# Attention and two feed-forward blocks on one core: the early weight decoding pinned in ScalarE's queue and paced, the turned operands of the second block begun later, one more piece behind the last product

## The chip, the cores and the metric

The kernel runs on one core of a Trainium2 chip. The metric is device time of one execution in microseconds (us), the median of several executions. Engine names in the rows: PE is TensorE's matmul, PEld its weight load, DVE is VectorE, ACT is ScalarE, POOL is GpSimd, SP is the engine whose queue issues nearly all DMAs here.

## What is computed

```python
# q, k, v: 4 batches x 8 heads x 576 positions x 64; window 128, one slope per head
scores = where(0 <= rel < 128, q @ k.T / sqrt(D) - slope * rel, -1e9)
attn   = softmax(scores) @ v                       # -> x: 2304 tokens x 512
y      = ((x @ w_a) * (x @ w_b)) @ w_out           # moe:  d_ff = 1536
h      = y @ w_in2                                 # moe2: d_ff = 2048
g      = where(h >= 1, h, where(h <= -1, 0, (h + 1)**2 / 4))
out    = g @ w_out2                                # 2304 x 512
```

The weights come as 64-bit numbers; the kernel turns each tile of them into float32 words on chip, and then into a high and a low part, so that three matmuls stand for one product.

## The kernel before

**Stages.** First the attention, with the first four of twelve column blocks of the first feed-forward block computed beside it, half a block of tokens (256) at a time: `attention()` yields after each step, `products()` after each group of three or twelve matmuls, and the loop at the end of the kernel runs them against each other by the table `PACE`. Then `after_attention()`: seven visits, a plain one that ends the first four column blocks for the last tokens, three visits for the other eight blocks of the first feed-forward block, and three for the second. In those six a product of 2x2 blocks is done as seven products (`seven_steps`), whose operands are sums of blocks of the tokens, made ahead by `x7_first` and `x7_second` ("turned"). The last visit splits its down product in seven too, but for its last pair of blocks, which is done plainly by `close7_pieces`.

**Early decoding.** Beside the attention, `early_job(key)` decodes 22 further weight tiles (`EARLY`), whose words go to memory until the later stages want them. `fetch` loads the raw tile (512 KB) on SP's queue. `words` then does two ACT instructions, `e = |high half|` and `up = low half * 2^-29`, and three DVE instructions; `total_bits` adds `e` and `up` on DVE, and a DMA stores `e` (256 KB, line 694). One step of a job runs with each step of `products()` (`WE = 1`), and a job has six. There are three buffers for raw tiles, two for `e` (`EB = 2`) and two for `up`; so the ACT instruction that writes `e` of a tile needs the store of the tile two before it to have landed, and a raw load needs the tile three before it to have been read. `fetch_next` keeps `FETCH` raw tiles on their way.

**Order.** In the attention stage a scheduler decides the order in each engine's queue, by priority and by when it takes inputs to be there. In the later stages PE's order is that of the code (`manual_schedule`), and the scheduler orders the other engines. Each queue runs in order: an instruction that waits holds up what stands behind it. `background` runs the later decoding and the turned operands beside the matmuls, one step of the latter after each product (`BG`), `after` lets out the pieces of the down products at a rate per product. In the last pair of the last visit that rate is lowered by `LAG / 7` a product, so that pieces are left over to stand between the last product and `close7_pieces`, which needs the last product's result.

**`x7_second`** makes the turned operands of the second block for one block of tokens, in two halves: a load of `xf` (line 928), then the first DVE subtraction on it (line 931), and further sums and splits.

Of the kernel before, what the change touches and what calls it, by code (L numbers as in the profile page):

```python
# [9 lines left out]
F32 = mybir.dt.float32  # L10
# [3 lines left out]
AF = mybir.ActivationFunctionType  # L14
# [12 lines left out]
def attention_and_two_ffns(  # L27
# [12 lines left out]
    nc = tc.nc  # L40
# [53 lines left out]
    YB = 4  # L94
    EARLY = 22
    EFROM = 1
    WE = 1
    HOLD = 3
    PRI = 300
    ET = mybir.EngineType  # L100
# [5 lines left out]
    BG = [(3, 2, 24), (3, 1, 24), (1.5, 1, 19), (2, 1, 12), (3, 1, 0), (3, 1, 0), (2, 1, 0)]  # L106
    VISITS = [(1, 0), (1, 1), (1, 2), (2, 0), (2, 1), (2, 2)]
    FLIP = [0, 1, 0, 0, 1, 0]
    FETCH = 2
    ABS = 'AA'  # L110
    D7 = ((2, 2),)
    GN = 11
# [5 lines left out]
    E_PC = 'V'  # L118
    E_W = 'P'
    CORD = ((1, 0), (0, 0), (0, 1), (1, 1))  # L120
    LAG = 2
    E_PV = 'V'
    TQ = 3
    TN = 3
    HP = lambda n: n < HPN
    const = ctx.enter_context(tc.tile_pool(name="const", bufs=1))
    xp = ctx.enter_context(tc.tile_pool(name="xp", bufs=1))
# [351 lines left out]
    state = {"w": 0, "credit": 0.0}  # L479
# [35 lines left out]
            count["e"] = count.get("e", 0) + 1  # L515
            fetch(coming.popleft(), "w64" if count["e"] % 3 or FETCH < 2 else "w64c")

    def words(key):

        pool, be, bu = (later["dec"], EB2, UB2) if later else (wdec, EB, UB)  # L520
        if key not in raws:
            fetch(key)
        raw = raws.pop(key)
        word = raw.bitcast(U32).rearrange("p (n two) -> p n two", two=2)
        lo, hi = word[:, :, 0], word[:, :, 1]
        e = pool.tile([P, 4 * P], U32, tag="e", name="e", bufs=be)
        up = pool.tile([P, 4 * P], U32, tag="up", name="up", bufs=bu)
        ef = e.bitcast(F32)
        if ABS[bool(later)] == "A":
            nc.scalar.activation(ef, hi.bitcast(F32), AF.Abs)  # L530
            yield e, up
        nc.scalar.activation(up, lo, AF.Copy, scale=2.0**-29)  # L532
        yield e, up
        if ABS[bool(later)] == "A":
            nc.vector.tensor_scalar(ef, ef, W64_MIN, W64_MAX, ALU.max, ALU.min)
        else:
            nc.vector.tensor_scalar(ef, hi.bitcast(F32), W64_MIN, W64_MAX, ALU.abs_max, ALU.min)
        yield e, up
        nc.vector.tensor_scalar(e, e, 5, 2, ALU.logical_shift_left, ALU.logical_shift_right)
        yield e, up  # L540
        nc.vector.scalar_tensor_tensor(e, hi, 0xC0000000, e, ALU.bitwise_and, ALU.bitwise_or)
        yield e, up
# [133 lines left out]
    V = nc.vector  # L676
# [10 lines left out]
    coming = deque(ahead)  # L687

    def early_job(key):
        for e, up in words(key):  # L690
            yield
        total_bits(e, e, up)
        early[key] = dram.tile([P, 4 * P], F32, name=f"w32_{key[0]}{key[1]}")
        nc.sync.dma_start(early[key], e.bitcast(F32))
        fetch_next()
        yield
# [198 lines left out]
    def x_tile(name):  # L895
        return xp.tile([P, 2, BW], F32R, tag="x", name=name, bufs=NB * NC)

    def x7_second(b, where):

        t1, t2 = two()  # L900
        xs[b] = [x_tile(f"z{c}") for c in range(NC)]
        if where == "memory":
            parked[2, b] = {q: dram.tile([P, 2, 2, QW], F32, name=f"t2_{b}{q}") for q in (2, 3, 6)}
        else:
            turned[2, b] = {q: t_tile(where) for q in (2, 3, 6)}

        def split(hi, lo, src):
            nc.scalar.copy(hi, src)
            yield
            minus(V, lo, src, hi)  # L910
            yield

        def turn(q, c, src):
            if where != "memory":
                yield from split(*(turned[2, b][q][:, z, c] for z in range(2)), src)
                return
            while not room():
                yield "no room"
            me = ("turned2", b, q, c)
            take(me)  # L920
            t = w_tile("wt")
            yield from split(t[:, 0, :QW], t[:, 1, :QW], src)
            nc.sync.dma_start(parked[2, b][q][:, :, c], t[:, :, :QW].bitcast(F32))
            give(me)

        for c in range(2):
            f = xp.tile([P, 2, BW], F32, tag="x", name="xf", bufs=NB * NC)
            nc.sync.dma_start(f, xf[b][:, c])
            yield
            b11, b12, b21, b22 = f[:, 0, Q1], f[:, 0, Q2], f[:, 1, Q1], f[:, 1, Q2]  # L930
            V.tensor_tensor(t1, b12, b11, less_)
            yield
            V.tensor_tensor(t2, b22, t1, less_)
            yield
            V.tensor_tensor(b12, b22, b12, less_)
            yield
            yield from turn(3, c, t1)
            yield from turn(2, c, t2)
            V.tensor_tensor(t1, b21, t2, less_)
            yield  # L940
            for k in range(2):
                x = xs[b][c + 2 * k]
                yield from split(x[:, 0], x[:, 1], f[:, k])
            yield from turn(6, c, t1)
        made.add((2, b))
        yield
# [576 lines left out]
    for need in products():  # L1523
# [7 lines left out]
        if not later and begun >= 0:  # L1531
            for _ in range(XE):
                if jobs_x:
                    run(jobs_x)
            if begun >= EFROM and ahead and not waiting and not jobs_w:
                jobs_w.append(early_job(ahead.pop(0)))
            for _ in range(WE):
                if jobs_w:
                    run(jobs_w)
        owed += PACE[min(begun, len(PACE) - 1)]  # L1540
# [33 lines left out]
```

## Time and profile before

| | |
|---|---|
| runs | 973.14, 975.70, 975.98 us; median 975.7 |
| the profiled execution's own time | 974.94 us |
| its span in the profile | 973.2 us, so 1.74 us lie outside the span |
| PE busy in the span | 937.1 us, 96% |
| DVE, ACT, POOL busy | 720.6, 565.0, 169.5 us |
| mean granted TensorE clock | 0.988 of 2.4 GHz |

A PE that is busy for 96% of the span can gain from a change only by its few idle stretches, and by those in which its clock is granted lower. The page's row by slices rounds both away, so stages are read by windows.

### The profile page before, as it was taken

The page shows a single profiled execution, that of the slowest core. Times are in us where ns is not written, and L with a number is a line of the kernel's source. Part 1 is how long each engine was busy: PE and PEld are TensorE (multiplying, and loading weights), DVE is VectorE, ACT ScalarE, POOL GpSimd, SP SyncE. Part 2 cuts the span into 40 slices and gives each one's busy share as a digit, 9 for nine tenths or more (in the row PEclk, how much of TensorE's full clock was granted, in tenths as well). Part 3 has the DMA queues.
Part 4 walks back from the last instruction along what each step waited for, and adds up shares of the span by engine and source line. Part 5 has one row for each costly group of instructions (what it writes and reads, how often), then busy time and mean ns, then how long its engine had stood idle before and what let it go on. Part 6 is the DMA issues. An engine that isn't in the chain of part 4 may idle for free.

```text
span 973.2 us, 18277 instructions
## 1 busy us (share of the span) xinstructions
PE 937.1 (96%) x6397; PEld 874.6 (90%) x6397; DVE 720.6 (74%) x1704; ACT 565.0 (58%) x1346; POOL 169.5 (17%) x311
## 2 busy tenths in 40 slices
PE   4999999899999999999999999999999999999997
PEld 3889889799999899999989999888888888899997
DVE  6698787794944988885677667899876656467886
ACT  6778676664433454353434435788775656586662
POOL 5567444344100000000000000000000000032233
PEclk9999999999999999999999999999999999999999
DMA  9967787830545888798868997876777776587851
GB/s 215 181 147 180 209 218 185 220 98 2 163 156 198 311 311 301 281 365 332 265 225 328 383 364 271 310 247 211 272 285 238 246 241 229 178 269 257 268 185 65
DMA packets 177580, 229.01 MB, mean 235 GB/s; under 512 B 92880, under 2 KB 132048, under 8 KB 177488
## 3 DMA queue, kind: packets, MB, share of 16 engines
q1 hardware_dynamic: 173680, 224.96, 70.9%
q10 hardware_dynamic: 3808, 2.88, 1.0%
q8 instruction: 51, 0.84, 0.3%
q14 instruction: 41, 0.34, 0.1%
HBM read 156.24 MB, written 71.57 MB: 234 GB/s over the span
## 4 chain that ended last, share of the span: by engine, by line
PE 71%; DVE 4%; DMA 3%; issue 1%; ACT 0%; SPq 0%; POOL 0%; DVEq 0%; POOLq 0%
PE mm L1027 32%; PE acc L1209 14%; PE acc L1148 10%; PE acc L1352 5%; PE mm L1117 3%; PE acc L642 1%; DMA xf<-xf 1%; DMA e<-w_b 1%; PE ps_s L348 1%; PE mm L593 1%; PE mm L595 1%; PE ps_o L412 1%; PE mm L594 1%; PE acc L1396 1%; PE ps_t L380 0%
## 5 line engine op out<-in xcount | busy, mean ns | idle before, releaser
L1256 POOL TENSOR_TENSOR h<-h,h 128x384 f32<-128x384 f32 x21 | 23.5, 1118 | 656.0 <-DVE h L1243 647.1
L1027 PE MATMUL mm<-xt,ws 128*128 128x384 f32 x612 | 124.5, 338 | 0.7 <-DVE a L968 0.7
L1027 PEld LDWEIGHTS mm<-xt,ws 128*128 128x128 f32 x612 | 106.8, 188 | 6.0 <-DVE a L968 1.3
L1027 PE MATMUL mm<-z,ws 128*128 128x384 f32 x480 | 97.2, 337 | 0.5 <-DVE h L968 0.5
L1027 PEld LDWEIGHTS mm<-z,ws 128*128 128x128 f32 x480 | 84.4, 188 | 5.3 <-DVE h L968 0.8
L1209 PE MATMUL acc<-ws,gh 128*128 128x512 f32 x252 | 79.0, 394 | 0.0
L369 POOL TENSOR_SCALAR s<-s,ssum 128x192 f32<-128x192 f32 (+2 forms) x144 | 69.8, 498 | 28.9 <-DVE ssum L364 20.9
L358 ACT ACTIVATE s<-s,nmax 128x192 f32<-128x192 f32 (+2 forms) x144 | 62.4, 437 | 16.2 <-DVE nmax L354 15.9
L1027 PE MATMUL mm<-x,ws 128*128 128x384 f32 x348 | 70.7, 338 | 0.3 <-ACT s L1048 0.2
L1148 PE MATMUL acc<-gh,ws 128*128 128x512 f32 (+1 forms) x224 | 65.3, 335 | 0.0
L1027 PEld LDWEIGHTS mm<-x,ws 128*128 128x128 f32 x348 | 61.7, 188 | 3.8 <-ACT s L1048 0.9
L530 ACT ACTIVATE e<-w 128x512 f32<-128x512 f32 x68 | 45.4, 672 | 33.8 <-DMA w_a<-e 6.3
L348 PE MATMUL ps_s<-kt,diag 128*128 128x192 f32 (+2 forms) x288 | 62.1, 337 | 2.0 <-ACT diag L176 0.9
L976 ACT CAST gh<-a 128x384 fp32r<-128x384 f32 x56 | 28.3, 513 | 56.8 <-DVE a L1056 37.9
L968 DVE TENSOR_TENSOR h<-mm,s 128x384 f32<-128x384 f32 x72 | 39.8, 553 | 27.7 <-PE mm L1027 27.6
L1352 PE MATMUL acc<-ws,go 128*128 128x256 f32 x423 | 58.9, 282 | 0.4 <-DVE sum L968 0.4
L593 PE MATMUL mm<-x,w 128*128 128x256 f32 x192 | 57.4, 304 | 0.1
L1352 PEld LDWEIGHTS acc<-ws,go 128*128 128x128 f32 x423 | 56.1, 189 | 1.5 <-DVE sum L968 1.3
L595 PE MATMUL mm<-x,w 128*128 128x256 f32 x192 | 57.0, 298 | 0.1
L532 ACT ACTIVATE up<-w 128x512 uint32<-128x512 uint32 x68 | 45.9, 675 | 19.2 <-DVE e L546 7.5
L594 PE MATMUL mm<-x,w 128*128 128x256 f32 x192 | 56.9, 297 | 0.0
L976 ACT CAST gh<-c 128x384 fp32r<-128x384 f32 x68 | 34.6, 512 | 37.4 <-PE acc L1209 29.9
(153 smaller groups left out, 2519.8 us busy)
## 6 DMA issues: line engine op xcount, KB each, us to landing
ws<-w_ii SPq DMA_DIRECT2D x57, 512.0 KB, 5.5
ws<-w_p SPq DMA_DIRECT2D x48, 512.0 KB, 4.5
ws<-w_ab SPq DMA_DIRECT2D x37, 512.0 KB, 6.3
w_p<-wb SPq DMA_DIRECT2D x30, 512.0 KB, 4.7
w<-in_moe_w_out_dram SPq DMA_DIRECT2D x28, 512.0 KB, 5.0
w_ab<-wb SPq DMA_DIRECT2D x24, 512.0 KB, 3.0
w_ii<-wb SPq DMA_DIRECT2D x24, 512.0 KB, 4.1
w<-in_moe_w_in_dram SPq DMA_DIRECT2D x16, 512.0 KB, 4.7
```

The lines of the kernel that those rows point to most:

```text
L348: nc.tensor.matmul(ps[:, z, c : 3 * D], qd[:, i - q0 // D, :], kt[:, (i - 2) * D + c - k0 : (i + 1) * D - k0], start=True, stop=True,)
L358: nc.scalar.activation(at(z, i), at(z, i), AF.Exp, bias=nmax[:, z : z + 1], scale=-1.0, accum_out=ssum[:, z : z + 1],)
L369: ENG[E_N[2 * b + (m >= 2)][z]].tensor_scalar(at(z, i), at(z, i), ssum[:, z : z + 1], 1.0, ALU.mult, ALU.mult)
L532: nc.scalar.activation(up, lo, AF.Copy, scale=2.0**-29)
L593: nc.tensor.matmul(ps, w[:, 0, cs], xh[c], start=(c == 0), stop=False)
L594: nc.tensor.matmul(ps, w[:, 0, cs], xl[c], start=False, stop=False)
L595: nc.tensor.matmul(ps, w[:, 1, cs], xh[c], start=False, stop=(c == NC - 1))
L976: nc.scalar.copy(hi[:, t_], src)
L1027: nc.tensor.matmul(ps, w[:, k, cs], operand(here, q, ci, m), start=q in (0, 1, 3) and ci + n == 0, stop=ci == 1 and n == 2, skip_group_che ...
L1148: nc.tensor.matmul(dst, w[:, i, cs], m[:, t_], start=first and k == 0 and (n < NC or c % 2 == 0), stop=last and k == 2 and (n < NC or c % ...
L1209: nc.tensor.matmul(v["acc"][n], m[:, ss], w[:, i], start=first and k == 0, stop=last and k == 2,)
L1352: nc.tensor.matmul(dst, g[a][:, ss], w[:, b], start=opens and n == 0, stop=closes and n == 2, skip_group_check=True,)
```

## The change

Four edits. **Pinned decoding:** the two ACT instructions of an early job are tied behind the instruction that the code issued to ACT just before (`keep_in_program_order`), so the scheduler can't place them ahead of it; one job step is run for three out of four steps of `products()` (`WE = 0.75`) in place of each; and `fetch_next` keeps three raw tiles on their way. The buffers stay three, two and two. **Later operands:** `x7_second` lets four products go by between the load of a half and the first subtraction on it, in place of one, and ties this subtraction behind what DVE was given before. **Closing pair:** `LAG` is 3, not 2.

```diff
-    WE = 1
+    WE = 0.75
-    FETCH = 2
+    FETCH = 3
-    LAG = 2
+    LAG = 3
+    PIN = True
+    XW = 4
+    PINX = True
...
-    def words(key):
+    def words(key, pin=lambda ins: ins):
...
-            nc.scalar.activation(ef, hi.bitcast(F32), AF.Abs)
+            pin(nc.scalar.activation(ef, hi.bitcast(F32), AF.Abs))
...
-        nc.scalar.activation(up, lo, AF.Copy, scale=2.0**-29)
+        pin(nc.scalar.activation(up, lo, AF.Copy, scale=2.0**-29))
...
-        for e, up in words(key):
+        for e, up in words(key, tc.keep_in_program_order if PIN else lambda ins: ins):
...
+    def pinned(ins):
+        return tc.keep_in_program_order(ins) if PINX else ins
...
             nc.sync.dma_start(f, xf[b][:, c])
-            yield
+            for _ in range(XW):
+                yield
...
-            V.tensor_tensor(t1, b12, b11, less_)
+            pinned(V.tensor_tensor(t1, b12, b11, less_))
...
-            for _ in range(WE):
+            state["thin"] = state.get("thin", 0.0) + WE
+            while state["thin"] >= 1.0:
+                state["thin"] -= 1.0
                 if jobs_w:
                     run(jobs_w)
```

**ACT's queue in the attention stage.** Before, from the softmax exponential (line 358) ahead of one early tile's `e` (line 530, tile `w64_2738`) to the next tile's `e` (`w64_2807`); line 532 is `up`, the others are evictions of the attention and of the products.

```order
L358 ACTIVATE s3_140,ssum_2533<-s3_140,nmax_2532 128x192
L530 ACTIVATE e_2826<-w64_2738 128x512
L176 CAST x11_111<-ps_o_2569 128x3x64
L176 CAST x11_111<-ps_o_2568 128x3x64
L622 CAST gh_2696<-a_sb_2652 128x256
L532 ACTIVATE up_2945<-w64_2807 128x512
L176 COPY pt_2663<-ps_t_2659 128x384
L176 CAST x21_115<-ps_o_2569 128x64
L176 CAST x21_115<-ps_o_2568 128x2x64
L358 ACTIVATE s0_134,ssum_2637<-s0_134,nmax_2636 128x64
L358 ACTIVATE s0_134,ssum_2637<-s0_134,nmax_2636 128x128
L530 ACTIVATE e_2944<-w64_2807 128x512
```

After the change, the two tiles that stand nearest to there (`w64_2716` and `w64_2838`); lines are three higher.

```order
L533 ACTIVATE e_2978<-w64_2716 128x512
L535 ACTIVATE up_2979<-w64_2716 128x512
L361 ACTIVATE s3_140,ssum_2946<-s3_140,nmax_2945 128x192 x2
L179 COPY pt_3009<-ps_t_3006 128x256
L361 ACTIVATE s0_134,ssum_2987<-s0_134,nmax_2986 128x192 x2
L625 CAST gh_3100<-a_sb_3028 128x256
L535 ACTIVATE up_3055<-w64_2838 128x512
L179 COPY pt_3046<-ps_t_3042 128x384
L533 ACTIVATE e_3054<-w64_2838 128x512
```

From one tile's `e` to the next there were two exponentials, and now there are four. Over all 22 tiles, the first `e` stood and stands behind exponential 54 of 144; the last stood behind exponential 119, and now stands behind the last, 144.

**DVE's queue where the second half of the first block's operands begins** (first feed-forward block, last of its visits). Before, line 931 stands ahead of the decoder's last sum (546), four sums into `xsum` and the two splits `gl` that PE's down product reads.

```order
L541 SCALAR_TENSOR_TENSOR e_6860<-w64_6858,e_6860 128x512
L1060 TENSOR_TENSOR a_6576<-mm_6534,a_6576 128x384
L1056 TENSOR_TENSOR a_6576<-a_6576,s1_6618 128x384
L931 TENSOR_TENSOR x32_6559<-xf_6864 128x384
L546 ISA e_6860<-e_6860,up_6861 128x1024
L968 TENSOR_TENSOR xsum_6498<-acc_5776,xsum_6498 128x512
L170 TENSOR_TENSOR gl_6648<-a_6576,gh_6647 128x384
L968 TENSOR_TENSOR xsum_6516<-acc_5777,xsum_6516 128x512
L933 TENSOR_TENSOR x32_6559<-xf_6864,x32_6559 128x384
L935 TENSOR_TENSOR xf_6864<-xf_6864 128x384
L170 TENSOR_TENSOR gl_6648<-a_6576,gh_6647 128x384
```

After the change the same place reads so (lines are seven higher here):

```order
L544 SCALAR_TENSOR_TENSOR e_6857<-w64_6855,e_6857 128x512
L1067 TENSOR_TENSOR a_6576<-mm_6534,a_6576 128x384
L1063 TENSOR_TENSOR a_6576<-a_6576,s1_6616 128x384
L549 ISA e_6857<-e_6857,up_6858 128x1024
L975 TENSOR_TENSOR xsum_6498<-acc_5776,xsum_6498 128x512
L173 TENSOR_TENSOR gl_6645<-a_6576,gh_6644 128x384
L975 TENSOR_TENSOR xsum_6516<-acc_5777,xsum_6516 128x512
L173 TENSOR_TENSOR gl_6645<-a_6576,gh_6644 128x384
```

The subtraction on the second load (now line 938) has gone 23 instructions further back. The first half's subtraction of the same block, 22 instructions ahead of this place, stands between the same instructions before and after.

**PE's queue at the last product** (line 1027, after it 1034), with the pieces of the seven-product down step (1352, after it 1359) and the first of the closing pair (1396, after it 1403). Before:

```order
L1027 MATMUL mm_11437<-xt_8902,ws_11326 128x384 x6
L1352 MATMUL acc_10338<-ws_11247,go_11396 128x256 x3
L1352 MATMUL acc_11587<-ws_11245,go_11396 128x256 x6
L1352 MATMUL acc_11595<-ws_11245,go_11396 128x256 x3
L1352 MATMUL acc_10336<-ws_11247,go_11426 128x256 x6
L1352 MATMUL acc_10338<-ws_11247,go_11426 128x256 x3
L1352 MATMUL acc_11611<-ws_11218,go_11391 128x256 x6
L1352 MATMUL acc_11619<-ws_11218,go_11391 128x256 x3
L1396 MATMUL acc_10337<-ws_11350,gh_11468 128x256 x2
```

After:

```order
L1034 MATMUL mm_11437<-xt_8902,ws_11326 128x384 x6
L1359 MATMUL acc_10335<-ws_11247,go_11396 128x256 x3
L1359 MATMUL acc_10338<-ws_11247,go_11396 128x256 x3
L1359 MATMUL acc_11587<-ws_11245,go_11396 128x256 x6
L1359 MATMUL acc_11595<-ws_11245,go_11396 128x256 x3
L1359 MATMUL acc_10336<-ws_11247,go_11426 128x256 x6
L1359 MATMUL acc_10338<-ws_11247,go_11426 128x256 x3
L1359 MATMUL acc_11611<-ws_11218,go_11391 128x256 x6
L1359 MATMUL acc_11619<-ws_11218,go_11391 128x256 x3
L1403 MATMUL acc_10337<-ws_11350,gh_11468 128x256 x2
```

Three matmuls of the down step have moved from ahead of the last product to behind it: 33 stand there now, 30 before.

## Rows read from the trace of the kernel before

**Rows 1.** Windows: busy us of each engine in a stretch, granted clock, DMA.

```profile
60.00:86.00 26.00, 23.94 (x229) 21.17 (x228) 23.98 (x78) 21.21 (x69) 18.80 (x34) 0.93 0.66 161
86.00:110.00 24.00, 24.00 (x271) 23.25 (x271) 21.32 (x75) 18.55 (x58) 15.23 (x28) 1.00 0.79 198
110.00:204.00 94.00, 82.98 (x885) 77.71 (x884) 74.32 (x248) 63.22 (x210) 39.63 (x91) 0.95 0.76 199
204.00:245.00 41.00, 41.00 (x521) 39.71 (x521) 24.85 (x100) 21.73 (x77) 17.90 (x47) 1.00 0.12 35
303.00:350.00 47.00, 46.08 (x260) 42.98 (x260) 36.60 (x75) 22.52 (x46) 0.00 (x0) 1.00 0.79 284
350.00:720.00 370.00, 366.95 (x1997) 341.34 (x1996) 290.26 (x583) 201.89 (x401) 0.00 (x0) 1.00 0.84 300
```

**Rows 2.** Timeline of PE, 108 to 123 us, its one stall.

```profile
116.88 2.06 PE L412 MATMUL ps_o<-pt,v 64*64 64x64 f32 x56 [2.02 <-ACT pt L176]
```

**Rows 3.** Timeline of ACT, 105 to 122 us.

```profile
111.25 0.67 ACT L530 ACTIVATE e<-w 128x512 f32<-128x512 f32 x1 [1.01 <-DMA w_a<-e]
...
115.35 0.66 ACT L530 ACTIVATE e<-w 128x512 f32<-128x512 f32 x1 [2.29 <-DMA w<-in_moe_w_a_dram]
...
116.48 0.35 ACT L176 COPY pt<-ps_t 128x256 f32<-128x256 f32 x1
```

**Rows 4.** ACT's waits from 60 to 225 us: total us, times, longest.

```profile
ACT e L530 <- DMA w_a<-e: 6.3, 4, 2.3
...
ACT e L530 <- DMA w_o<-e: 4.9, 4, 1.7
ACT up L532 <- DMA w<-in_moe_w_out_dram: 3.9, 2, 3.0
ACT e L530 <- DMA w<-in_moe_w_a_dram: 3.9, 2, 2.3
ACT e L530 <- DMA w_b<-e: 2.6, 3, 1.7
ACT e L530 <- DMA w<-in_moe_w_b_dram: 2.4, 1, 2.4
...
ACT up L532 <- DMA w<-in_moe_w_b_dram: 1.9, 1, 1.9
...
ACT up L532 <- DMA w<-in_moe_w_a_dram: 1.0, 2, 0.7
```

**Rows 5.** DMA issues, 60 to 225 us: count, KB each, median us to landing.

```profile
w<-in_moe_w_a_dram SPq DMA_DIRECT2D x8, 512.0 KB, 4.9
...
w_a<-e SPq DMA_DIRECT2D x8, 256.0 KB, 3.7
```

**Rows 6.** SP's waits, 60 to 225 us: a raw load, and the first later load.

```profile
SPq L710 <- DVE pt L178: 23.1, 1, 23.1
SPq L508 <- DVE e L541: 18.8, 7, 5.3
```

**Rows 7.** Chain that ended last, 300 to 336 us: start, us, what.

```profile
310.12 4.89 DMA e<-w_b
```

**Rows 8.** Timeline of DVE, 480 to 514 us: the two halves' first subtraction.

```profile
494.60 0.56 DVE L931 TENSOR_TENSOR x<-xf 128x384 f32<-128x384 f32 x1 [2.33 <-DMA xf<-xf]
...
506.70 0.56 DVE L931 TENSOR_TENSOR x<-xf 128x384 f32<-128x384 f32 x1 [0.81 <-DMA xf<-xf]
```

**Rows 9.** Timeline of PE, 484 to 512 us: its stalls.

```profile
497.21 1.33 PE L1027 MATMUL mm<-xt,ws 128*128 128x384 f32 x6 [0.73 <-DVE a L968]
...
510.99 0.50 PE L1148 MATMUL acc<-gl,ws 128*128 128x512 f32 x1 [1.47 <-DVE gl L170]
```

**Rows 10.** Timeline of PE, 938 to 974 us: behind the last product.

```profile
955.54 3.75 PE L1352 MATMUL acc<-ws,go 128*128 128x256 f32 x30
959.12 0.40 PE L1396 MATMUL acc<-ws,gh 128*128 128x256 f32 x2
960.77 0.39 PE L1396 MATMUL acc<-ws,gl 128*128 128x256 f32 x1 [1.25 <-DVE gl L170]
```

## The prediction

> **What bounds the kernel now.** PE does. I read the table of engines first, then windows by stage, then inside the stages what PE waited for, and last the waits of the engine that it waited for. In the stages from 350 us on PE stands idle for 3 us in 370 [rows 1]; nothing that shortens work on another engine pays there. The attention stage is different, and the windows cut it so that the reason shows. From 60 to 86 us and from 110 to 204 us PE is idle for 2.06 and 11.02 us, and its granted clock is 0.93 and 0.95 of 2.4 GHz. Between them, from 86 to 110 us, it has no idle time and a clock of 1.00, though the early decoding runs there at its full pace and DVE is 89% busy (21.32 of 24). From 204 to 245 us, with no early decoding left, it also has none [rows 1]. So neither the attention nor the amount of decoding holds PE up, but something that happens in some places of the decoding.
>
> What it is can be read at one stall. At 114.9 us PE waits 2.02 us for an eviction `pt` of ACT [rows 2]. ACT had been standing since 113 us at the `e` of an early tile, for its raw load, 2.29 us; that `pt` comes only behind it [rows 3]. At 111.25 us it had stood 1.01 us for a store, that of the tile two before, since `e` has two buffers [rows 3]. Summed over 60 to 225 us ACT waits 8 times for raw loads (3.9 + 3.9 + 2.4 + 1.9 + 1.0 = 13.1 us) and 11 times for stores (6.3 + 4.9 + 2.6 = 13.8 us) [rows 4], 26.9 us in all. PE pays twice: it stands still, and its clock is granted lower behind such a stop.
>
> What is there to be had: 13.1 us of idle time, and for the clock 0.07 x 26 + 0.05 x 94 = 6.5 us (a stretch at half of 2.4 GHz does half its work; the clocks have two decimals, so 0.6 us either way). Together 19.6 us.
>
> **Pinned decoding: raw loads.** Nothing is added or removed: the same 22 tiles, the same two ACT and four DVE instructions each, the same DMAs. What moves is seen in the queues. I count in softmax exponentials, which stand in every queue's order; 65 of them lay between the first and the last early tile, over the 118 us from 86 to 204 us, 1.8 us each. From the point where a raw buffer has been read to the first instruction on the tile that comes into it next there were 5.0 exponentials on the mean of 19 pairs, and there are 9.7 after: 9 us become 17 us. The load itself lands 4.9 us after its issue [rows 5], and before it SP stands up to 5.3 us for the buffer [rows 6]: 10 us, more than the 9 and well under the 17. I take the waits for raw loads as gone. Shared by wait time they are 13.1 of 26.9, so 9.5 us of the 19.6.
>
> **Pinned decoding: stores.** A store lands 3.7 us after its issue [rows 5]. From the sum that it stores to the `e` that waits for it there were 3.0 exponentials on the mean of 20 pairs, 4 or fewer in 19 of them; after there are 4.8, and 4 or fewer in 10. About half of the stores' share of 10.1 us goes, 5.0 us. Here a rule of the Trainium skill speaks against the change. The row shows ACT waiting at the same instruction eleven times for the same kind of thing [rows 4]. The page Perfetto Trace Analysis (Identifying Performance Opportunities, Optimization Strategy) says that the same gap repeating over a stretch can mean that there is not enough room for the next tile, buffers that is; the change adds none, so by it all the store waits would stay, and the sum for this stage would be 9.5 and not 14 us. No row shows `e` with three buffers. That the repeated gap sits on two `e` buffers agrees with the rule; that 86 to 110 us runs without loss on the same two [rows 1] says that distance does as well as buffers.
>
> The two shares make 14.5 us. Clock stretches come whole, so I take 14. Bounds: nothing below, if each wait is only replaced by another; 19.6 us above.
>
> **What the pace costs.** The last of the 22 sums, which stood long ahead of the attention's end (the last tile's `e` behind exponential 119 of 144), now stands on DVE just ahead of the attention's last splits, about five tiles in a stretch that had none. DVE was 61% busy there [rows 1], so they are hidden. What is late next is the first later decoding: its load stands on SP for the end of the attention, 23.1 us before [rows 6], and behind the last store it will also wait for that to land, up to 3.7 us [rows 5] less the splits that run meanwhile. From there a serial chain of decodings leads to the first visit of the seven-product stage; its transfers lie on the chain that ended last [rows 7], and PE already waits 0.9 us there (47.00 - 46.08, 303 to 350 us [rows 1]), so a late start is paid in full. I take 1 us, from 0 to 3.
>
> **Later operands.** DVE stands 2.33 us and then 0.81 us at the first subtraction of a half, for its load [rows 8]; PE waits 0.73 us in the first place and 1.47 us in the second [rows 9]. The queue's order shows that only the second moves: its subtraction stands 23 instructions further back, and the two `gl` that PE waited for go ahead of it. The first stands where it stood, with the same load ahead of it. I take 1.4 us of the 1.47; bounds 0 and 2.2 us, both stalls. The six further yields make 37 steps of 31, over the 56 products of a visit at one step each, so no operand comes too late for its visit, and nothing is run in a heap. The last block's halves go back by a whole visit, to places where PE has no idle time to lose or win.
>
> **Closing pair.** Behind the last product 30 matmuls take 3.75 us, and then PE stands 1.25 us for the last product's `gl` [rows 10]. Three more stand there now, 3 x 3.75 / 30 = 0.4 us, so the last product ends that much earlier and its `gl` too. I take 0.4 us; bounds 0 and the whole 1.25.
>
> **Sum.** -14 + 1 - 1.4 - 0.4 = -14.8 us. Against the profiled execution's own 974.94 us that is 960.1; that execution lies 0.76 us under the median of the runs shown, so 960.9 as a median, about **961 us**. All bounds on the good side make -19.6 - 2.2 - 1.25, 952.7 us as a median.
>
> **Rivals.**
> - *The store waits stay* (two `e` buffers decide): only the 9.5 us of the raw loads and the small terms, -9.5 + 1 - 1.4 - 0.4, so 965.4 us. For it: eleven waits, and the nine shortest distances of after are no longer than those of before. Against it: half of the distances are longer by 2 exponentials or more.
> - *The loads don't come earlier* (the third load has no new buffer, and SP stands at the buffer as before, 18.8 us in 7 waits [rows 6]): the raw waits stay, half of the store waits go, -5.0 + 1 - 1.4 - 0.4, so 969.9 us. Against it: the doubled distance.
> - *The stalls only change their name*: with ACT free, DVE holds the chain of scores, exponential and sum, being 92% busy from 60 to 86 us [rows 1]; what is won there is lost behind it, and the time is about 975 us. Against it: 86 to 110 us, where DVE's 89% cost PE nothing.
> - *Slower: the later decoding starts late.* The decoding of the early tiles runs over the attention's end, and the chain of the later tiles, paid in full at 303 to 350 us, starts behind it. It decides from a delay of 16 us on, which is what the other terms give; at 20 us the time is 974.94 - 15.8 + 20 + 0.76 = 979.9 us. Against it: the order, where the last sum stands ahead of the attention's last splits.
>
> **How the numbers follow.** The forecast has 0.60, the store waits 0.17, the loads 0.08, the changed name 0.09, the late start 0.06. A difference of under 0.3%, 2.9 us, is no more than what runs of this kernel differ by. The first three are faster by more than that, 0.85; the fourth is the same, 0.09; the fifth slower, 0.06. The range goes from 953 (all good bounds) to 971 us, which takes in the first three cases and leaves out the last two, 0.15, and a little at the lower end; the forecast's own range is 955 to 966.
>
> **What would show it.** Right: from 60 to 204 us PE's idle time falls from 13.1 us to under 5, the clock there is 0.97 or more; ACT's waits for raw loads at line 533 or 535 are gone, those for stores (`w_a<-e` and its like) come to 7 us or less; the end of the attention comes some 14 us earlier, and the later stages last as long as before, but for 1.5 us less near 500 us and 0.4 us less at the end. Wrong: PE stalls behind `pt` in the attention stage as often as before with ACT idle ahead of a decoding instruction (the stores or the loads), or with ACT idle ahead of an exponential (DVE); or a gap of PE of some us between the attention's end and the first seven-product visit.

## The result: 963.1 us, ratio 0.9874, and the profile after

Six executions of the changed kernel took 959.26 to 964.24 us, median 963.06; six of the kernel before, on the same chips, 972.74 to 975.98, median 973.71. The ratio is 0.9874, 95% interval 0.9854 to 0.9894: faster by 12.3 us (10.3 to 14.2). The ratio is not the quotient of the two medians: they differ by 10.65 us (0.9891), which lies inside the interval. The forecast was 961 us against a median of 975.7, 14.7 us less. The profiled execution of the changed kernel is one of the longer ones, 963.82 us with a span of 962.0; against the profiled 974.94 it is 11.1 us shorter.

The windows of [rows 1], now of the changed kernel (stretch, busy us of PE, PEld, DVE, ACT, POOL, then the granted clock and the DMA share):

```profile
60.00:86.00 26.00, 23.53 (x192) 20.27 (x192) 21.59 (x75) 18.62 (x62) 17.06 (x31) 0.87 0.65 146
86.00:110.00 24.00, 24.00 (x288) 23.10 (x287) 18.99 (x61) 17.10 (x59) 14.23 (x30) 1.00 0.59 138
110.00:204.00 94.00, 91.79 (x1051) 87.68 (x1050) 78.63 (x276) 68.53 (x232) 50.92 (x108) 1.00 0.75 189
204.00:245.00 41.00, 40.27 (x462) 38.85 (x462) 35.25 (x108) 24.28 (x73) 16.04 (x33) 1.00 0.52 171
303.00:350.00 47.00, 45.62 (x259) 42.66 (x258) 41.23 (x86) 22.87 (x47) 0.00 (x0) 1.00 0.86 310
350.00:720.00 370.00, 368.29 (x1996) 341.91 (x1995) 281.52 (x563) 199.05 (x396) 0.00 (x0) 1.00 0.82 295
```

From 110 to 204 us PE's idle time has gone from 11.02 to 2.21 us and the clock from 0.95 to 1.00. From 60 to 86 us nothing is better: 2.47 us idle against 2.06, and a clock of 0.87 against 0.93. That stretch is one of the places where the forecast was wrong, as the experiments show. The stretch from 204 us, which had no idle time, now has 0.73 us.

ACT's waits from 60 to 225 us, at the decoding's two instructions (total us, times, longest), to be read against [rows 4]:

```profile
ACT e L533 <- DMA w_a<-e: 2.3, 2, 1.3
ACT e L533 <- DMA w_b<-e: 2.3, 1, 2.3
...
ACT up L535 <- DMA w<-in_moe_w_a_dram: 1.8, 1, 1.8
ACT up L535 <- DMA w<-in_moe_w_out_dram: 1.3, 1, 1.3
ACT e L533 <- DMA w_o<-e: 1.0, 2, 0.9
...
ACT up L535 <- DMA w<-in_moe_w_b_dram: 0.7, 1, 0.7
```

The waits for stores have gone from 13.8 to 5.6 us, those for raw loads from 13.1 to 3.8. PE's waits for an eviction `pt` of ACT, from 86 to 204 us, before and after:

```profile
PE ps_t L380 <- ACT pt L176: 5.4, 3, 3.0
PE ps_o L412 <- ACT pt L176: 2.6, 2, 2.0
```

```profile
PE ps_t L383 <- ACT pt L179: 0.3, 1, 0.3
PE ps_o L415 <- ACT pt L179: 0.2, 1, 0.2
```

The timeline of PE from 120 to 135 us holds the longest stall left between 86 and 204 us; it waits for the exponentials that POOL scales, no longer behind an eviction of ACT as in [rows 2]:

```profile
128.62 0.33 PE L383 MATMUL ps_t<-ident,s 128*128 128x128 f32 x1 [1.25 <-POOL s L372]
```

SP's queue from 225 to 250 us shows the end of the early decoding (the last store of line 697) and the first later load (line 713), which in the kernel before was issued at 243.58:

```profile
235.03 0.32 SPq L697 DMA_DIRECT2D w_a<-e  x1
...
237.18 0.33 SPq L713 DMA_DIRECT2D w<-w_a  x1
```

The attention's last `ps_o` matmul ends at 234.3 us, in the kernel before at 243.4: 9.1 us earlier. The first later load is 6.4 us earlier, so against the attention it has lost 2.7 us.

In the visit whose later half was moved, the first half's subtraction waits as in [rows 8] and PE behind it as in [rows 9]; the stall at `gl` near 511 us has no answer in this timeline of PE from 480 to 505 us, and near 500 us none of DVE's rows waits for a second half. First DVE, then PE:

```profile
486.33 0.56 DVE L938 TENSOR_TENSOR x<-xf 128x384 f32<-128x384 f32 x1 [2.07 <-DMA xf<-xf]
```

```profile
488.94 1.32 PE L1034 MATMUL mm<-xt,ws 128*128 128x384 f32 x6 [0.47 <-DVE a L975]
490.44 1.33 PE L1034 MATMUL mm<-x,ws 128*128 128x384 f32 x6 [0.18 <-ACT s L1055]
```

And the tail, PE from 940 to 955 us, for [rows 10]: 33 matmuls behind the last product. The wait of 1.25 us for the last `gl` is gone, and there is one of 0.37 us for a sum of DVE:

```profile
944.62 4.11 PE L1359 MATMUL acc<-ws,go 128*128 128x256 f32 x33
948.57 0.40 PE L1403 MATMUL acc<-ws,gh 128*128 128x256 f32 x2
...
950.51 0.50 PE L1403 MATMUL acc<-ws,gh 128*128 128x256 f32 x2 [0.37 <-DVE sum L975]
```

### The profile page after: what moved, and what is told of

Its sections match the earlier page's. It is cut to its first block, busy times and chain, and to the rows that moved or that the text cites. A ratio compares the mean times of both kernels' runs of the same rounds, so it can differ in the third digit from the quotient of the medians.

```text
span 962.0 us, 18278 instructions
## 1 busy us (share of the span) xinstructions
PE 936.5 (97%) x6397; PEld 874.1 (91%) x6397; DVE 724.4 (75%) x1704; ACT 563.8 (59%) x1346; POOL 174.9 (18%) x311
## 4 chain that ended last, share of the span: by engine, by line
PE 77%; DVE 9%; DMA 8%; ACT 3%; issue 1%; POOL 1%; SPq 0%; DVEq 0%; POOLq 0%; ACTq 0%
PE mm L1034 33%; PE acc L1216 14%; PE acc L1155 10%; PE acc L1359 5%; PE ps_s L351 3%; PE mm L1124 2%; PE ps_o L415 2%; DMA e<-w_b 1%; PE acc L645 1%; PE ps_t L383 1%; PE mm L597 1%; PE mm L596 1%; PE mm L598 1%; ACT s L361 1%; DMA w_o<-e 1%
## 5 line engine op out<-in xcount | busy, mean ns | idle before, releaser
L361 ACT ACTIVATE s<-s,nmax 128x192 f32<-128x192 f32 (+2 forms) x144 | 62.3, 436 | 15.6 <-DVE nmax L357 14.1
```

The source lines that it names most:

```text
L361: nc.scalar.activation(at(z, i), at(z, i), AF.Exp, bias=nmax[:, z : z + 1], scale=-1.0, accum_out=ssum[:, z : z + 1],)
```

## The experiments

A theory and its rivals: **distance** (the gain comes from more work between a tile's release and the next use of its buffer), **buffers** (two `e` buffers are the limit), **pin** or **pace** or **third load** alone, and **density** (how closely the decoding is packed beside the attention, whatever its waits). Distances are means in softmax exponentials from the queues' order, as in the prediction: store 3.0 and raw 5.0 before, 4.8 and 9.7 after.

The table has every run's ratio to the kernel before on the same chip (95% interval), and three readings of its profile from 86 to 204 us: PE's idle time (118 us less PE's busy time); the stage's loss, which is this plus (1 - granted clock) x 118 us; and ACT's waits at the decoding's two instructions, for stores and for raw loads.

| kernel | ratio | PE idle | loss | store waits | raw waits |
|---|---|---|---|---|---|
| before | 1 | 11.0 | 15.7 | 13.8 | 9.6 |
| changed | 0.9874 (0.9854 to 0.9894) | 2.2 | 2.2 | 5.6 | 0 |
| decode_only | 0.9912 (0.9895 to 0.9929) | 3.4 | 4.5 | 7.0 | 0 |
| xw_only | 0.9991 (0.9977 to 1.0005) | 9.6 | 13.1 | 11.4 | 7.8 |
| lag_only | 0.9997 (0.9983 to 1.0011) | 10.8 | 10.8 | 10.5 | 9.9 |
| pin_only | 0.9983 (0.9967 to 0.9999) | 8.1 | 11.7 | 11.8 | 0 |
| pin_we | 0.9917 (0.9901 to 0.9933) | 2.8 | 2.8 | 5.8 | 0 |
| we_fetch | 1.0038 (1.0020 to 1.0055) | 12.1 | 15.6 | 15.1 | 5.4 |
| before_pt6 | 1.0058 (1.0040 to 1.0075) | 13.5 | 20.6 | 16.1 | 8.0 |
| before_eb3_pt6 | 1.0118 (1.0102 to 1.0134) | 13.0 | 24.8 | 2.6 | 10.3 |
| after_eb3_pt6 | 0.9883 (0.9868 to 0.9899) | 2.8 | 2.8 | 0 | 2.6 |
| after_eb3_we1 | 0.9978 (0.9962 to 0.9994) | 7.3 | 12.0 | 5.3 | 0 |
| after_we065 | 0.9886 (0.9861 to 0.9911) | 2.7 | 3.9 | 0.6 | 0 |
| before_noearly | one time, 980.26 us | 1.1 | 1.1 | 0 | 0 |

The readings are of one execution each. In `xw_only` and `lag_only` the queues of PE, ACT, DVE and POOL stand in the attention in the same order as in the kernel before, so these three rows show what one order's readings differ by from execution to execution: idle time 9.6 to 11.0 us, store waits 10.5 to 13.8, raw waits 7.8 to 9.9, and the loss 10.8 to 15.7, most of it by the clock (1.00, 0.97 and 0.96 of 2.4 GHz). The attention's end differs too: 240.7, 241.7 and 243.4 us. A loss that differs by less than some 5 us shows nothing by itself; the ratios decide there. The windows from 86 to 204 us of `lag_only`, `pin_only`, `pin_we`, `after_eb3_pt6` and `after_eb3_we1`, in this order:

```profile
86.00:204.00 118.00, 107.17 (x1199) 100.76 (x1195) 99.54 (x333) 84.22 (x277) 58.34 (x125) 1.00 0.78 205
86.00:204.00 118.00, 109.88 (x1199) 105.10 (x1199) 93.62 (x328) 83.72 (x275) 57.44 (x123) 0.97 0.75 192
86.00:204.00 118.00, 115.17 (x1329) 110.44 (x1326) 97.34 (x339) 84.61 (x287) 63.14 (x136) 1.00 0.74 183
86.00:204.00 118.00, 115.19 (x1336) 110.91 (x1336) 97.28 (x349) 87.17 (x298) 60.99 (x137) 1.00 0.76 183
86.00:204.00 118.00, 110.73 (x1218) 106.18 (x1217) 94.52 (x329) 84.30 (x285) 61.09 (x128) 0.96 0.78 193
```

**The three parts apart.** In `decode_only`, `xw_only` and `lag_only` one part of the change is done and the others are as before.

```diff
 decode_only:  PIN = True   WE = 0.75  FETCH = 3    (LAG = 2, XW = 1, PINX = False)
 xw_only:      XW = 4       PINX = True             (the rest as before)
 lag_only:     LAG = 3                              (the rest as before)
```

> The pinned, paced decoding with three loads ahead, without the later operands and without the larger LAG. Theory (the distances in ACT's queue give nearly the whole gain): PE's idle time from 86 to 204 us stays at some 2 us against 11 before, the three low-clock stretches of 110 to 204 us are gone, and the time is 10 to 11 us under the kernel before, ratio 0.989 to 0.990. Rival (the parts add to each other beyond their sum, or the gain sits in the later stages): less than 8 us, ratio above 0.992.

> The later operands alone. Theory: the 1.47 us stall of PE near 510 us goes, the 0.73 us one near 497 us stays, nothing else moves, so 1.0 to 1.5 us less, ratio 0.9985 to 0.999. Rival (the load is late next at another place, or the stall was hidden by slack behind it): no difference, ratio 1.000, with a stall of the same size in another place of the same visit.

> The larger LAG alone. Theory: three more matmuls stand behind the last product, the wait for the last gl falls from 1.25 us to about 0.85 us, and the time by 0.4 us, ratio 0.9996, which these runs can hardly tell from none; the profile's tail tells it. Rival (DVE's order at the end counts, not the three matmuls): the wait falls by more than 0.4 us.

The decoding gave 8.6 us (6.9 to 10.2), a little less than the theory said; it holds most of the gain. The other two give 0.9 us (from 2.2 less to 0.5 more) and 0.3 us (from 1.7 less to 1.1 more), each within what these runs can tell from none. By the ratios the three sum to 9.8 us against 12.3 for the whole, by the differences of the medians to 11.2 against 10.7; the intervals meet, so no part is shown to add to another. What the profiles show of the two small ones is sharper than the times. In `xw_only` PE is idle for 1.08 us from 350 to 720 us, before for 3.05, so its stall has not moved to another place. Its timeline of PE from 470 to 515 us: the stall at `mm<-xt` stays, and the one at `gl` is gone:

```profile
495.53 1.33 PE L1034 MATMUL mm<-xt,ws 128*128 128x384 f32 x6 [0.66 <-DVE a L975]
497.03 1.33 PE L1034 MATMUL mm<-x,ws 128*128 128x384 f32 x6 [0.17 <-ACT s L1055]
```

In `decode_only`, where this part is as before, it is there, 1.55 us in the same kind of row:

```profile
502.02 0.50 PE L1155 MATMUL acc<-gl,ws 128*128 128x512 f32 x1 [1.55 <-DVE gl L173]
```

Of `lag_only`, the tail of PE is that of the changed kernel, a wait of 0.37 us:

```profile
953.90 4.11 PE L1359 MATMUL acc<-ws,go 128*128 128x256 f32 x33
...
959.78 0.50 PE L1403 MATMUL acc<-ws,gh 128*128 128x256 f32 x2 [0.37 <-DVE sum L975]
```

So the rival of this run holds: PE waits 0.88 us less there, more than the 0.4 of three matmuls, and no longer for `gl`. That DVE's order is the rest is read from these rows; no run changed the order alone. Before, in DVE's timeline from 955 to 962 us, the `gl` that PE waited for was the instruction that took 2.18 us:

```profile
958.08 0.55 DVE L1070 SCALAR_TENSOR_TENSOR c<-h,c 128x384 f32<-128x384 f32 x1
958.54 2.18 DVE L170 TENSOR_TENSOR gl<-c,gh 128x384 fp32r<-128x384 f32 x1
```

In the changed kernel (DVE from 925 to 962 us) `gl` stands one place earlier, takes 0.55 us, and the slow place falls to `c`:

```profile
947.19 0.55 DVE L173 TENSOR_TENSOR gl<-c,gh 128x384 fp32r<-128x384 f32 x1
947.66 2.20 DVE L1077 SCALAR_TENSOR_TENSOR c<-h,c 128x384 f32<-128x384 f32 x1
```

**Pin, pace and third load.** Which of the three edits of the decoding is it?

```diff
 pin_only:  PIN = True                            (WE = 1,    FETCH = 2)
 pin_we:    PIN = True    WE = 0.75               (           FETCH = 2)
 we_fetch:  PIN = False   WE = 0.75   FETCH = 3
```

> The pin alone, at the old pace and with two loads ahead. By the queue's order the mean distance from a raw buffer's last read to its next use is 7.0 exponentials (5.0 before, 9.7 after), that from a sum to the e that waits for its store 3.1 (3.0 before, 4.8 after). Theory (distances decide): about two fifths of the raw loads' share and none of the stores', 2 to 5 us less, ratio 0.995 to 0.998. Rival (the pin itself decides, since it keeps ACT from taking a decoding instruction ahead of the attention's): 9 to 11 us less, ratio 0.989 to 0.991.

> Pin and pace, with two raw loads ahead in place of three. The order of ACT and DVE is that of the whole change (raw distance 9.7, store distance 4.8 exponentials). Theory (distances decide, the third load ahead hardly counts): 9 to 11 us less than before, ratio 0.989 to 0.991. Rival (the third load ahead is what makes the loads early): raw waits stay at some 10 us and the time is at most 6 us under before, ratio above 0.994.

> The lower pace and three loads ahead, without the pin. The order hardly differs from before (raw distance 5.1, store distance 3.0 exponentials): unpinned, the scheduler puts the decoding's ACT instructions back to where they stood. Theory (distances decide): within 2 us of before, ratio 0.998 to 1.002. Rival (the pace or the third load decides): 5 to 10 us less, ratio 0.990 to 0.995.

Neither half does it. The pin alone gives 1.7 us (0.1 to 3.2); pace and third load without the pin cost 3.7 us (2.0 to 5.4). Pin and pace together give 8.1 us (6.5 to 9.6), the same as with the third load, which so does nothing that can be measured. The order says why: unpinned, the lower pace leaves the distances at 3.0 and 5.1, since the scheduler puts the ACT instructions back where they stood; only pinned does the pace become spacing. That `we_fetch` would come within 2 us of before was a miss. Its store and raw waits are 20.5 us and its loss that of before, but the profiled execution, 974.68 us, is a short one of this kernel (median 977.20), so the profile can't show where the 3.7 us lie. Two smaller misses: `pin_we` gave a little less than the 9 to 11 us of its theory, and the pin alone took away all the raw waits, not two fifths of them, and yet gave 1.7 us where 2 to 5 were expected.

`pin_only` also prices the raw waits. Of ACT's waits from 86 to 204 us in it, those for stores are these, and there is none for a raw load:

```profile
ACT e L533 <- DMA w_b<-e: 5.2, 4, 2.4
ACT e L533 <- DMA w_a<-e: 4.9, 4, 2.7
...
ACT e L533 <- DMA w_o<-e: 1.7, 2, 1.4
```

The raw waits (7.8 to 9.9 us in the three rows of the old order) are gone, the store waits are what they were (11.8 us), and the time fell by 1.7 us (0.1 to 3.2); the stage's loss, 11.7 us, is within the spread of the old order. From there to `pin_we` the store waits fall by 6.0 us, the loss by 8.9 and the time by another 6.4. A us of raw wait was worth less than a us of what the pace removes.

**Is it the buffers?** A third `e` buffer, for which one of the seven `pt` buffers makes room, on the kernel before and on the changed one; and the control with six `pt` alone.

```diff
 before_pt6:       PT = 6                (kernel before)
 before_eb3_pt6:   PT = 6   EB = 3       (kernel before)
 after_eb3_pt6:    PT = 6   EB = 3       (changed kernel)
```

> The kernel before with three e buffers in place of two (room for it comes from pt, six buffers in place of seven); no pin, the old pace, two loads ahead. The store distance becomes 4.5 exponentials (3.0 before, 4.8 after), the raw distance stays at 5.4. Rule to be tested (a repeated gap means too few buffers): the store waits of ACT, 13.8 us, fall under 4 us and the time by about 5 us, ratio 0.995. By distances: the same 4 to 6 us, since the buffer is one way to lengthen them, and the raw waits stay at some 13 us. Rival (the raw loads alone hold PE up): less than 2 us, ratio above 0.998.

> The kernel before with six pt buffers in place of seven and two e buffers as before: the control for the third e buffer, which made the kernel before 11.5 us slower, ratio 1.0118. Theory (six pt buffers are too few beside a decoding that runs at its full pace): ratio 1.008 to 1.013, with ACT waiting some 10 us at pt for PE as it does with three e buffers. Rival (the third e buffer itself does it, since it lets the decoding run in a denser stretch: between exponentials 49 and 103 in place of 54 and 119): ratio 0.998 to 1.003.

> The changed kernel with three e buffers (pt six in place of seven). The store distance becomes 8.8 exponentials, the raw distance 9.4. Theory (the 5.6 us of store waits that are left in the changed kernel still cost PE something): 1 to 3 us less than the changed kernel, ratio to before 0.985 to 0.987. Rival (what PE still waits for in the attention is DVE's chain, not the decoding): the same as the changed kernel, 0.987 to 0.988; if six pt buffers are too few, longer than it.

The third buffer does what it should to the wait and not to the time. The store waits fall from 16.1 us (`before_pt6`) to 2.6, and the ratio goes from 1.0058 to 1.0118. So six `pt` buffers cost 0.58% (less than the theory of that run said, more than its rival), and the third `e` buffer another 0.6%. The Trainium skill's rule (Perfetto Trace Analysis, Identifying Performance Opportunities, Optimization Strategy), that a gap which repeats on the engine that should be saturated can mean too few buffers, fits the place of the wait, though ACT is not that engine here, PE is. The measurement decides against it as a remedy here, beside six `pt` buffers: the gap went from 16.1 to 2.6 us, the time grew by 0.6%. No run has three `e` buffers beside seven of `pt`. The windows of `before_eb3_pt6` show where it went:

```profile
86.00:204.00 118.00, 105.05 (x1062) 98.74 (x1062) 93.71 (x317) 83.17 (x268) 54.57 (x114) 0.90 0.75 201
```

PE is idle for 13.0 us (13.5 in `before_pt6`), and the clock is granted at 0.90 (0.94 there). The decoding now runs between exponentials 49 and 103, where it ran from 54 to 114 with two buffers, and the raw waits are as long as ever, 10.3 us. In the changed kernel the third buffer takes the 5.6 us of store waits away altogether, and the time stays (0.9883 against 0.9874), less what six `pt` may cost there, which was not measured.

**The pace by itself, and lower still.**

```diff
 after_eb3_we1:  PT = 6   EB = 3   WE = 1       (changed kernel otherwise)
 after_we065:    WE = 0.65                      (changed kernel otherwise)
```

> The changed kernel with three e buffers and six pt buffers, at the old pace of one decoding step for each step of the products. Store distance 6.0 and raw distance 6.4 exponentials (4.8 and 9.7 in the changed kernel). Theory (pace counts because it gives the raw loads time, and the stores are covered here by the buffer): raw waits of 5 us or more come back, ratio 0.990 to 0.994. Rival (pace counts because it keeps DVE and ACT free for the attention, so a denser decoding loses whatever its distances are): ratio above 0.994. Third (with the pin, either pace does once e has three buffers): 0.987 to 0.989.

> The changed kernel at a still lower pace, 0.65: only 19 of the 22 tiles are decoded beside the attention by its end, the other three are decoded in the later stages; raw distance 10 to 12 and store distance about 6 exponentials. Theory (in the changed kernel the distances are nearly long enough, and the last tiles now pay in the later stages): within 2 us of the changed kernel, ratio to before 0.986 to 0.990. Rival (the store waits that are left are worth their share, and the later stages hide three more decodings): 2 to 4 us less than it, ratio 0.983 to 0.986. Rival (late decoding is paid in full, as the prediction's slower rival has it): ratio above 0.991, with a new stall of PE between 290 and 350 us.

Between `after_eb3_we1` and `after_eb3_pt6` only the pace differs: 0.9978 and 0.9883, 9.3 us. ACT's decoding waits differ by less than 3 us (5.3 and 2.6), and the changed kernel has no fewer than those 5.3 us (5.6) with a loss of 2.2 us where this one loses 12.0. So the rival of that run holds: the old pace loses here though ACT waits no longer at the decoding than in the changed kernel. That the closer packing does it is what is left, not shown by itself; six `pt` buffers beside the old pace are the other candidate, and against them stands that ACT waits for PE to give back a `pt` no longer than in `after_eb3_pt6` (6.7 against 9.0 us). PE then waits for DVE. The waits of PE, and then of DVE, from 86 to 204 us in `after_eb3_we1`:

```profile
PE ps_o L415 <- DVE nmax L357: 4.2, 2, 2.4
```

```profile
DVE y L181 <- DMA x2p<-y: 7.7, 3, 3.1
DVE e L538 <- ACT e L533: 5.3, 4, 3.3
```

One such stall followed, in the timelines of DVE and PE from 125 to 200 us: an eviction of `y` on DVE stands 2.77 us for the store of the `y` before it, and PE 2.44 us for the maximum that DVE makes behind it:

```profile
134.23 0.69 DVE L181 COPY y<-acc 128x512 f32<-128x512 f32 x1 [2.77 <-DMA x2p<-y]
```

```profile
135.25 1.66 PE L415 MATMUL ps_o<-pt,v 64*64 64x64 f32 x28 [2.44 <-DVE nmax L357]
```

At the pace of 0.65 (19 tiles of 22 done by the attention's end) the attention ends at 229.2 us, 5.2 us before that of the changed kernel, and the time is not better: 0.9886. Two new stalls, of 0.88 us just ahead of 390 us and 1.35 us ahead of 398, are part of what the later stages pay back. The late start in full (a ratio above 0.991) did not come.

```profile
390.00 1.28 PE L1034 MATMUL mm<-xt,wb 128*128 128x384 f32 x6 [0.88 <-DMA xt<-t]
398.04 1.30 PE L1034 MATMUL mm<-xt,wb 128*128 128x384 f32 x6 [1.35 <-DVE xsum L975]
```

**What the attention loses without any early decoding.** No tile is decoded early; the later stages do the work (and pay for it), so only the attention is read.

```diff
 before_noearly:   EARLY = 0     (kernel before)
```

> The kernel before with no tile decoded beside the attention beyond the twelve of the first four column blocks; the 22 are decoded in the later stages, nothing is left out. Only the attention is looked at. Theory (PE's loss from 60 to 86 us belongs to the twelve tiles, which the change does not touch, so the prediction counted it wrongly into what was to be had): from 60 to 80 us PE has idle time of 1.5 to 2.5 us and ACT waits for raw loads there as before, and from 86 us to the attention's end it has less than 2 us of idle time at a clock of 0.98 or more. Rival (the early decoding causes both): no idle time above 0.5 us from 60 to 86 us. Third (the attention stalls by itself, without the decoding): idle time of 5 us or more from 86 us on.

Its windows from 60 to 86 and from 86 to 204 us:

```profile
60.00:86.00 26.00, 22.88 (x203) 20.00 (x202) 23.80 (x74) 19.43 (x63) 17.00 (x31) 0.93 0.57 127
86.00:204.00 118.00, 116.94 (x1369) 113.62 (x1368) 69.34 (x298) 72.14 (x274) 54.58 (x149) 1.00 0.38 77
```

And ACT's timeline there, with the decoding of the last of the twelve tiles of the first four column blocks (in the attention line 557 is theirs alone, and its last row is this one):

```profile
62.64 0.68 ACT L532 ACTIVATE up<-w 128x512 uint32<-128x512 uint32 x1 [1.84 <-DMA w<-in_moe_w_out_dram]
...
89.03 0.62 ACT L557 CAST w<-e 128x512 fp32r<-128x512 f32 x1 [2.01 <-DVE e L546]
```

The theory holds on both sides: from 60 to 86 us PE has lost as much as ever (3.1 us idle, clock 0.93), with ACT waiting for raw loads; from 86 us on 1.1 us. So of the loss from 86 to 204 us (10.8 to 15.7 us in three executions) all but some 1.1 us belongs to the early decoding, and of the loss from 60 to 86 us nothing.

## Why the prediction was right, and where its sizes were not

**The place and the kind of cause** were right: the gain is in the attention stage (9.1 of the 11.1 us between the profiled executions by its end), PE's waits behind ACT's `pt` fell from 8.3 to 0.5 us, the raw waits of the early tiles are gone, the store waits are about half (5.6 us against 10.5 to 13.8 in the three executions of the old order). 963.06 us lies in the forecast's own range.

**That the time came within some 2 us is in part luck.** The forecast started from a median of 975.7 us for the kernel before, which was 973.71 in the runs beside the result; the gain is 12.3 us by the ratio and 10.65 by the medians, where 14.7 were forecast. The decoding, -14 and +1 us in the sum, gave 8.6 by itself (6.9 to 10.2): this term was too large by about half. The attention was to end some 14 us earlier and ended 9.1 us earlier, or 6.4 and 7.4 against the other two executions of the old order.

**"What there is to be had ... together 19.6 us" was too large.** It counted the stretch from 60 to 86 us, 2.06 us idle and 1.8 us of clock. The tiles decoded there are the last of the twelve of the first four column blocks, which the change does not touch; the early ones begin at about 85 us. Three of the eight raw waits of [rows 4], 3.5 of 13.1 us, are theirs too, and in the changed kernel they are still there, 3.8 us. What was to be had is the loss from 86 to 204 us, 15.7 us in this profile and 10.8 in that of `lag_only`, less the 1.1 of `before_noearly`.

**Shared by wait time, the two terms were 9.5 and 5.0 us; that step failed.** By `pin_only` the raw waits were worth 1.7 us of time (0.1 to 3.2); the pace that came on top, 6.4. That part is not the store waits as such: `before_eb3_pt6` took them away and gained nothing, and `after_eb3_we1` has those of the changed kernel and loses 12.0 us. What is left is the spacing of the decoding, of which the shorter store wait is one sign. So the term of the raw loads was 7.8 us too large and the other 1.4 us too small, and only in part did the errors make up for each other: pin and pace give 8.1 us (6.5 to 9.6), beside the 13 forecast.

**What the pace costs, 1 us:** the size is about right, the cause not shown. In the changed kernel's profile PE has 0.46 us more idle time from 303 to 350 us (1.38 against 0.92), and the 0.73 us from 204 to 245 us are new; but `pin_only`, at the old pace, has 1.42 and 1.20 us in these stretches. The 0.73 us, and the lower clock from 60 to 86 us (0.87; `decode_only` had the 0.93 of before, and `lag_only`, with the old order, 0.87), take back a part of the 13.5 us by which the loss from 86 to 204 us fell between the two profiled executions; 9.1 us are left at the attention's end.

**Later operands, 1.4 us:** the stall of 1.47 us is gone and the one at the first half stands, as forecast; the time, 0.9 us, is known to no better than 1.4 us. **Closing pair, 0.4 us:** PE's wait there fell by 0.88 us, not 0.4, as `gl` also moved ahead of a slow instruction. From the first matmul of the seven-product down step to PE's last it is 112.3 us in the profiles of `lag_only` and of the changed kernel, and 112.8 to 112.9 in those of `before`, `xw_only`, `decode_only` and `pin_only`: 0.5 us, where the ratio of `lag_only` says 0.3, with 1.4 either way.

**The rivals.** *The store waits stay*: they fell to 5.6 us, and the buffer that was tried did not help. *The loads don't come earlier*: SP stands longer for the raw buffer than before (32.1 us in 12 waits against 18.8 in 7 [rows 6]), and yet no early tile waits for its load, because the next use has moved further off; `pin_we`, with two loads ahead, has no such wait either, so the third load is not what did it. *The stalls change their name* did not happen in the changed kernel, but it is what happens at the old pace in `after_eb3_we1`. *Slower, by a late start*: the first later load lost 2.7 us against the attention, far from the 16 that it needed.

**What stays open:** why `we_fetch` is slower than the kernel before; how much of the third buffer's loss in `before_eb3_pt6` comes by the closer packing and how much by the raw waits that remain; whether it is the closeness of the decoding alone that costs the 9.3 us in `after_eb3_we1`; and where the whole gain and the sum of its parts differ (by 2.5 us in the ratios, by -0.5 in the medians), which the intervals let be nothing.

## What to carry to other kernels

Before a loss is divided among causes, check for each stretch that the work the change touches runs in it: the same line served tiles that the change left alone. Read the same stretch in a second execution before a difference in it is given a cause: here one order of the queues lost 10.8 us in one and 15.7 in another. A us of wait on an engine off the bottleneck has no fixed price on the bottleneck; one experiment that removes a single kind of wait prices it, sharing by wait time doesn't. Where background work stalls a queue at its buffers, spreading it over the time there is can beat a further buffer, which lets it run closer together and moves the wait; and where a scheduler decides the order, as here, the pace became spacing only with the instructions pinned.

## What the runs showed of the hardware

The granted clock was not the same for the same work: with the attention's queues in the same order and 10.8 and 11.0 us of idle time from 86 to 204 us, it was 1.00 of 2.4 GHz in `lag_only` and 0.96 in the kernel before.

A DVE instruction of one shape took 0.55 us in one place of the tail and 2.2 us one place later, whichever instruction stood there (`gl` before, `c` after). POOL's timeline of the changed kernel, 930 to 966 us, has its four sums in that place:

```profile
947.35 8.23 POOL L1372 TENSOR_TENSOR sum<-sum,sum 128x768 f32<-128x768 f32 x4 [9.83 <-DVE sum L975]
```

The slow place begins at 947.66, just behind POOL's start at 947.35. The Trainium skill (Perfetto Trace Analysis, Optimizing Scalar/DVE Operations) says that GpSimd and VectorE share a read port of SBUF; the trace agrees with it in these rows, 0.55 against 2.20 us, and no run here moved POOL's sums to show it. Not every DVE instruction is slow beside POOL: two sums into `sum`, of which one operand is PE's accumulator, take the same time behind POOL's start as ahead of it (DVE of the changed kernel):

```profile
946.25 1.02 DVE L975 TENSOR_TENSOR sum<-acc,sum 128x512 f32<-128x512 f32 x2 [0.51 <-PE acc L1359]
...
949.78 1.01 DVE L975 TENSOR_TENSOR sum<-acc,sum 128x512 f32<-128x512 f32 x2
```

For the order of this tail it means that `gl`, on the critical path, should stand ahead of POOL's start.
